# Crossbar keys, whole-tile stores and one more half group in an attention and feed-forward kernel

## The chip, the cores and the metric

One core of a Trainium2 chip. The metric is the device time of one execution in microseconds (us), median of several; a profiled execution's span is 1.7 to 2.1 us shorter than its time. TensorE is PE in the views, VectorE DVE, ScalarE ACT, GpSimd POOL; SP issues most stores and all turns by the crossbar (DMA transposes). A turn is a transposition; SBUF and PSUM are the memories that the kernel's tiles lie in. A transfer is cut into packets that up to 16 DMA engines carry, and the packet records show closing packets of 4 bytes, read here as one for each engine that takes part in a store (16 in the kernel before, where over the tail, from 234.6 to 239.0 us, 14.7 store packets moved at a time in the mean).

## The reference

```python
# attention: q, k, v are (8 batches, 8 heads, 576, 64); k and v are averaged over groups of 8 rows
k_p = k.reshape(B, H, 72, 8, D).mean(axis=3)
v_p = v.reshape(B, H, 72, 8, D).mean(axis=3)
attn = softmax(q @ k_p.T / 8)
x = (attn @ v_p).transpose(0, 2, 1, 3).reshape(4608, 512)
# feed-forward: w1, w2, w3 are (512, 768), w_out is (768, 512)
out = np.maximum(np.maximum(x @ w1, x @ w2), x @ w3) @ w_out     # (4608, 512) float32
```

## The kernel before

The feed-forward part runs in nine blocks of 512 tokens. A block yields control after each group of four matmuls ("slot"), and a plan says which attention steps of a later batch go into which slot. Query rows are held in nine interleaved groups, so a tile of 128 tokens is two groups of 64 rows, each of which goes to every ninth row of the output.

```python
NG = 9
GS = (0, 2, 4, 6, 8, 1, 3, 5, 7)          # order of the row groups in a batch
...
def turn_k(b):                             # keys: transposed by TensorE, copied out of PSUM
    pkt = keys(b, TR)                      # six TensorE transposes
    for par in range(2):
        fill_kz(b, par, 0, H, pkt,
                nc.scalar.copy if b == 1 else nc.vector.tensor_copy)
...
# x of batches 2 to 7 and q of batches 2 to 7 are turned by the crossbar, issued from SP
nc.sync.dma_start_transpose(out=xT[:, :, g0 + keep:g0 + 128], in_=...)
nc.sync.dma_start_transpose(out=qTs[b], in_=...)
...
# project(): one tile of 128 tokens leaves in two stores of 64 rows
for u in range(2):
    b, g = divmod(2 * m + u, NG)
    dst = out[S * b:S * b + S, :].rearrange("(r g) c -> r g c", g=NG)
    (nc.scalar if last and u else nc.sync).dma_start(
        out=dst[:, GS[g], c], in_=osb[64 * u:64 * u + 64, c])
...
# block 0 takes its columns in parts (first weight group, end, first column, end column)
parts = [(0, 1, 0, 128), (0, 1, 128, 256), (1, 2, 0, 256), (0, 2, 256, NB), (2, JCH, 0, NB)]
```

The softmax here doesn't subtract the row's maximum and nothing guards it: scores larger than these inputs give would overflow.

Of the kernel before, what the change touches and what calls it, by code (L numbers as in the profile page):

```python
# [14 lines left out]
def kernel(  # L15
# [11 lines left out]
    nc = tc.nc  # L27
    dt = mybir.dt
    F32, BF16, F16 = dt.float32, dt.bfloat16, dt.float16

    B, H, S, D = q.shape
# [10 lines left out]
    NG = 9  # L42
    GS = (0, 2, 4, 6, 8, 1, 3, 5, 7)
    NR = 64
    KCH = C // 128
    JCH = DFF // 128
    TOK = B * S
    NB = 512
# [4 lines left out]
    sb2 = ctx.enter_context(tc.tile_pool(name="sb2", bufs=2))  # L53
# [1 line left out]
    psp = ctx.enter_context(tc.tile_pool(name="psp", bufs=1, space=PSUM))  # L55
    ctx.enter_context(tc.manual_schedule())

    kts, vts, qbs, kps, qTs, ets = {}, {}, {}, {}, {}, {}

    def after(loads, first):  # L60
        for x in loads:
# [49 lines left out]
    for i in range(3):  # L111
# [6 lines left out]
        out=wo_sb, in_=moe_w_out.rearrange("(jc p) c -> p jc c", p=128))  # L118
# [25 lines left out]
    def fold_k(b, e, i0=0, i1=6):  # L144
        if b not in kps:
            new_kp(b)
        fold(e, kts[b][:, i0:i1], [kps[b][:, i0:i1, i, :] for i in range(2)])
# [12 lines left out]
    def turn_q(b, n0, n1, evac, tag):  # L160
        if b not in qTs:
            qTs[b] = sb2.tile([128, 2 * NG, 128], BF16, name="qT", tag="qT")
        pqt = psp.tile([128, n1 - n0, 128], BF16, name="pqt", tag=tag[0],
                       bufs=tag[1])
        qf = qbs[b].rearrange("p hp t d -> p (hp t d)")
        for n in range(n0, n1):
            nc.tensor.transpose(pqt[:, n - n0, :], qf[:, 128 * n:128 * n + 128],  # L167
                                ident)
        evac(out=qTs[b][:, n0:n1, :], in_=pqt)

    def keys(b, tag):
        pkt = psp.tile([128, 6, 96], BF16, name="pkt", tag=tag[0], bufs=tag[1])
        for i in range(6):
            nc.tensor.transpose(pkt[:, i, :], kps[b][:, i, :, :], ident[0:96, 0:96])  # L174
        return pkt

    def fill_kz(b, par, h0, h1, pkt, evac):
        rows = slice(64 * par, 64 * par + 64)
        evac(out=kz_all[b % 2][rows, par, h0:h1, 0:Sp].rearrange(  # L179
                 "p h (r i) -> p h r i", i=6),  # L180
             in_=pkt[rows, :, 12 * h0:12 * h1].rearrange("p i (h r) -> p h r i", r=12))

    def turn_k(b):
        pkt = keys(b, TR)
        for par in range(2):
            fill_kz(b, par, 0, H, pkt,
                    nc.scalar.copy if b == 1 else nc.vector.tensor_copy)

    def pool_k(b, tag):

        new_kp(b)
        pkp = psp.tile([128, 6, D], F32, name="pkp", tag=tag[0], bufs=tag[1])
        for j in range(4):
            nc.tensor.matmul(pkp, identh[0:96, :], k16[:, :, j, :],
                             start=(j == 0), stop=(j == 3))
        nc.vector.tensor_copy(out=kps[b][:, :, 0, :], in_=pkp[0:96])
        nc.scalar.copy(out=kps[b][:, :, 1, :], in_=pkp[0:96])
# [12 lines left out]
    def new_et(b):  # L210
        ets[b] = sb2.tile([Sp, H, S], F16, name="et", tag="et")

    def scores(b, h):
        psc = psp.tile([128, 1024], F32, name="psc", tag="att", bufs=2)
        score(b, h, psc[:, 0:320], 0, 0, 5)
        score(b, h, psc[:, 320:512], 1, 0, 3)
        score(b, h, psc[:, 512:576], 1, 3, 4)
        exp(ets[b][:, h, :], psc[0:Sp, 0:S])
# [33 lines left out]
    TR = ("tr", 1)  # L252
# [5 lines left out]
    def do(b, steps):  # L258




        for name in steps.split():
            i = int(name[1:] or 0)
            if name[0] in "qQ":
                turn_q(b, *QS[i], nc.vector.tensor_copy if name[0] == "Q"
                       else nc.scalar.copy, TR)
            elif name[0] == "T":
                qTs[b] = sb2.tile([128, 2 * NG, 128], BF16, name="qT", tag="qT")
                nc.sync.dma_start_transpose(  # L270
                    out=qTs[b], in_=qbs[b].rearrange("p hp t d -> p (hp t d)"))
            elif name[0] == "k":
                turn_k(b)
            elif name[0] == "K":
                pool_k(b, PW)
            elif name[0] == "a":
                nc.vector.tensor_tensor(out=k16, in0=kts[b][:, :, 0:4],
                                        in1=kts[b][:, :, 4:8], op=ALU.add)
            elif name[0] == "s":
                if i == 0:  # L280
                    new_et(b)
                scores(b, i)
            elif name[0] == "v":
                xns[b, i] = values(b, CHUNKS[i][0])
            else:
                turn_x(b, *CHUNKS[i], xns[b, i], TR,
                       nc.vector.tensor_copy if name[0] == "X" else nc.scalar.copy)
# [23 lines left out]
    def hidden(n, hT):  # L311

        parts = [(0, JCH, 0, NB)]
        if n == 0:
            parts = [(0, 1, 0, 128), (0, 1, 128, 256), (1, 2, 0, 256), (0, 2, 256, NB),
                     (2, JCH, 0, NB)]
        elif n == 1:
            parts = [(0, 1, 0, 256), (0, 1, 256, NB), (1, JCH, 0, NB)]
        for j0, j1, c0, c1 in parts:
            for jc in range(j0, j1):  # L320
                yield from hidden_part(n, jc, c0, c1, hT)

    def project(n, hT):
        for mm in range(4):
            m = 4 * n + mm
            last = m == TOK // 128 - 1
            osb = sb3.tile([128, C], F32, name="osb", tag="osb", bufs=5)
            for c in ((slice(0, C // 2), slice(C // 2, C)) if last else (slice(0, C),)):
                po = psp.tile([128, c.stop - c.start], F32, name="po", tag="pw", bufs=3)
                for jc in range(JCH):  # L330
                    nc.tensor.matmul(po, hT[:, jc, bass.ts(mm, 128)], wo_sb[:, jc, c],  # L331
                                     start=(jc == 0), stop=(jc == JCH - 1))
                if c.start:
                    nc.vector.tensor_copy(out=osb[:, c], in_=po)
                else:
                    nc.scalar.copy(out=osb[:, c], in_=po)  # L336
                for u in range(2):
                    b, g = divmod(2 * m + u, NG)
                    dst = out[S * b:S * b + S, :].rearrange("(r g) c -> r g c", g=NG)
                    (nc.scalar if last and u else nc.sync).dma_start(  # L340
                        out=dst[:, GS[g], c], in_=osb[64 * u:64 * u + 64, c])
            yield

    def new_hT():
        return sb2.tile([128, JCH, NB], F16, name="hT", tag="hT")
# [13 lines left out]
    for i in range(0, 6, 2):  # L359
        src = kts[0][:, i:i + 2] if i else kt0  # L360
        f = const.tile([96, 2, 4, D], F32, name="kf", tag="kf")
# [5 lines left out]
            out=kps[0][:, i:i + 2].rearrange("p i a d -> p a i d"),  # L367
# [64 lines left out]
    def block(n, plan):  # L432

        hT = new_hT()
        slot = 0
        for part in (hidden(n, hT), project(n, hT)):
            for _ in part:
                if slot == 0 and n > 0:
                    pool_work(n, mms[-1])
                for b, steps in plan.get(slot, ()):  # L440
                    if b < B:
                        do(b, steps)
                slot += 1

    fold_v(1)
    fold_k(2, nc.gpsimd)
    block(0, {0: [(0, "X1")], 3: [(0, "v2")], 5: [(0, "v3")], 6: [(0, "x2")],
              8: [(0, "x3")], 10: [(0, "v4")], 12: [(0, "x4")],
              13: [(1, "a")], 15: [(1, "K")], 17: [(1, "k")], 19: [(1, "Q0")],
              20: [(1, "Q1")], 21: [(1, "Q2 s0")], 22: [(1, "Q3 s1")],  # L450
              23: [(1, "s2 s3")], 24: [(1, "s4 s5")], 25: [(1, "s6 s7")],
              26: [(1, "v0")], 27: [(1, "v1 x0"), (2, "T")], 28: [(1, "v2 x1")],
              29: [(1, "v3 x2")], 30: [(1, "v4")]})


    def plan(n):
        b, i = n + 1, 3 * (n == 1)
        got = {0: [], 3: [], 3 + i: [(b, "k")]}
        got.update({5 + i + h: [(b, f"s{h}")] for h in range(H)})
        got[12 + i].append((b + 1, "T"))  # L460
        got.update({15 + i + c: [(b, f"v{c} x{c}")] for c in range(5)})
        if n == 1:
            got[0].append((1, "x3"))
            got[3].append((1, "x4"))
        return got

    def pool_work(n, mm):

        if n + 2 < B:
            after([load_k(n + 2)], mm)  # L470
            load_q(n + 2)
            load_v(n + 2)
        if n == 1:
            fold_v(2)
        if n + 2 < B:
            fold_k(n + 2, nc.gpsimd)
            fold_v(n + 2)
# [33 lines left out]
```

## Time and profile before

| | before |
|---|---|
| time, median of 3 | 242.86 us (242.78 to 244.19) |
| span of the profiled run | 241.0 us |
| block 0 / block 3 / block 7 | 31.7 / 24.4 / 20.7 us |
| last matmul to the end of the span | 4.4 us |

The lines that carry this stand in the prediction. A "block" here goes from its first feed-forward matmul to the next block's. TensorE is busy all through blocks 1 to 8 (24.28 of 24.28 us in block 2, 20.72 of 20.72 in block 7), so nothing but its own instructions bounds them.

### The profile page before, as it was taken

How to read it: one execution, taken by the hardware profiler on the slowest of the kernel's cores; microseconds unless marked ns; L12 is line 12 of the kernel's file. 1: busy time of each engine (PE TensorE's matmuls, PEld its weight loads, DVE VectorE, ACT ScalarE, POOL GpSimd, SP SyncE). 2: the span in 40 equal slices, each digit the busy share in tenths (PEclk: the TensorE clock that was granted, in tenths of full speed). 3: DMA queues.
4: the chain of work that ended last, by engine and by line, in shares of the span. 5: the costliest groups of instructions: out<-in, count | busy, mean ns of one | idle time of the engine just before them, and what ended most of it. 6: DMA issues, size and time to landing. Idle time of an engine off the chain costs nothing.

```text
span 241.0 us, 4221 instructions
## 1 busy us (share of the span) xinstructions
PE 230.9 (96%) x1609; PEld 122.7 (51%) x1609; DVE 131.7 (55%) x239; ACT 100.1 (42%) x173; POOL 123.7 (51%) x91
## 2 busy tenths in 40 slices
PE   7698999999999999999999999999999999999992
PEld 3376555575554555455545554555455544444441
DVE  6856754665583558354836483648364834504530
ACT  2373247546513651365235523552355232142121
POOL 8864276989997479638880979286500000000000
PEclk9999999999999999999999999999999999999999
DMA  7999999999948995699769987997640253043006
GB/s 135 188 198 206 196 202 208 169 166 241 184 97 153 222 166 120 128 194 197 131 125 156 227 176 133 193 192 135 133 93 0 69 123 85 3 108 66 0 20 154
DMA packets 51939, 34.29 MB, mean 142 GB/s; under 512 B 32144, under 2 KB 46480, under 8 KB 51920
## 3 DMA queue, kind: packets, MB, share of 16 engines
q0 software_dynamic: 17088, 17.11, 45.5%
q1 hardware_dynamic: 34672, 16.79, 34.3%
q8 instruction: 12, 0.20, 0.3%
q10 hardware_dynamic: 160, 0.13, 0.2%
q14 instruction: 7, 0.06, 0.1%
HBM read 34.60 MB, written 9.44 MB: 183 GB/s over the span
## 4 chain that ended last, share of the span: by engine, by line
PE 89%; DVE 5%; ACT 2%; DMA 2%; issue 1%; DVEq 0%
PE pw L295 55%; PE po L331 19%; PE psc L203 6%; PE pav L238 4%; DMA kt<-in_k_dram 2%; PE pxt L229 1%; DVE kf L362 1%; ACT et L208 1%; DVE t L304 1%; PE pkt L174 1%; PE pvp L156 1%; DVE xn L246 1%; PE pqt L167 1%; DVE kp L366 1%; DVE kf L364 1%
## 5 line engine op out<-in xcount | busy, mean ns | idle before, releaser
L295 PE MATMUL pw<-xT,mw 128*128 128x512 f16 (+2 forms) x696 | 155.6, 364 | 0.8 <-ACT xT L233 0.7
L295 PEld LDWEIGHTS <-mw 128*128 128x128 f16 x696 | 61.8, 98 | 56.2 <-issue 1.0
L304 DVE TENSOR_TENSOR t<-t,pw 128x512 f16<-128x512 f16 (+2 forms) x58 | 37.8, 651 | 71.0 <-PE pw L295 43.7
L301 ACT CAST t<-pw 128x512 f16<-128x512 f32 (+2 forms) x58 | 32.3, 556 | 56.1 <-PE pw L295 54.8
L331 PE MATMUL po<-mwo,hT 128*128 128x512 f16 (+1 forms) x222 | 50.7, 373 | 0.0
L208 ACT ACTIVATE et<-psc 72x576 f16<-72x576 f32 (+2 forms) x62 | 40.7, 662 | 20.9 <-PE psc L203 20.7
L307 DVE TENSOR_TENSOR hT<-t,pw 128x512 f16<-128x512 f16 (+2 forms) x58 | 37.7, 650 | 9.0 <-PE pw L295 5.3
L336 ACT COPY osb<-po 128x512 f32<-128x512 f32 (+1 forms) x36 | 20.9, 580 | 47.7 <-PE po L331 43.7
L135 POOL TENSOR_TENSOR half<-vt 72x2048 f32<-72x2048 f16 x7 | 28.4, 4060 | 10.0 <-DMA vt<-in_v_dram 9.9
L331 PEld LDWEIGHTS <-hT 128*128 128x128 f16 x222 | 20.3, 97 | 21.3 <-DVE hT L307 2.4
L135 POOL TENSOR_TENSOR half<-kt 96x1536 f32<-96x1536 f16 x6 | 18.5, 3085 | 23.4 <-DMA kt<-in_k_dram 23.3
L246 DVE TENSOR_TENSOR xn<-pav,rcp 128x512 f16<-128x512 f32 x39 | 27.0, 691 | 1.5 <-DVE rcp L244 0.2
L136 POOL TENSOR_TENSOR half<-half 72x1024 f32<-72x1024 f32 (+1 forms) x13 | 27.2, 2096 | 1.0
L203 PE MATMUL psc<-qT,kz 128*128 128x64 bf16 (+3 forms) x192 | 25.9, 246 | 0.4 <-DVE kz L179 0.3
L203 PEld LDWEIGHTS <-kz 128*128 128x128 bf16 x192 | 17.8, 98 | 15.7 <-DVE kz L179 1.5
L238 PEld LDWEIGHTS <-et 72*128 72x128 f16 x312 | 15.2, 98 | 7.6
L238 PE MATMUL pav<-vp,et 72*128 72x65 f16 x312 | 16.5, 194 | 0.0
L244 DVE RECIPROCAL rcp<-pav 128x8 f32<-128x8 f32 x39 | 7.9, 204 | 9.4 <-PE pav L238 9.3
L139 POOL TENSOR_TENSOR kp<-half 96x384 bf16<-96x384 f32 x12 | 11.7, 993 | 0.5
L179 DVE COPY kz<-pkt 64x576 bf16<-64x576 bf16 (+1 forms) x14 | 9.9, 711 | 2.9 <-PE pkt L174 2.7
L79 POOL DMA_DIRECT2D vt<-in_v_dram x10 | 8.0, 804 | 2.9 <-DMA qb<-in_q_dram 2.2
L139 POOL TENSOR_TENSOR vp<-half 72x512 f16<-72x512 f32 x7 | 8.9, 1268 | 0.5
(48 smaller groups left out, 79.1 us busy)
## 6 DMA issues: line engine op xcount, KB each, us to landing
out_dram<-osb SPq DMA_DIRECT2D x70, 128.0 KB, 2.4
kt<-in_k_dram POOLq DMA_DIRECT2D x7, 576.0 KB, 7.4
qb<-in_q_dram POOLq DMA_DIRECT2D x7, 576.0 KB, 12.2
vt<-in_v_dram POOLq DMA_DIRECT2D x7, 576.0 KB, 15.0
mw<-in_moe_w_dram POOLq DMA_DIRECT2D x9, 256.0 KB, 9.3
mwo<-in_moe_w_out_dram POOLq DMA_DIRECT2D x1, 768.0 KB, 18.1
qb<-in_q_dram POOLq DMA_DIRECT2D x2, 288.0 KB, 7.0
xT<-xn SPq DMA_TRANSPOSE x30, 2.4
```

Source lines behind the costliest of these rows:

```text
L135: e.tensor_tensor(out=f, in0=t[:, :, 0:4, :], in1=t[:, :, 4:8, :], op=ALU.add)
L136: e.tensor_tensor(out=f[:, :, 0:2, :], in0=f[:, :, 0:2, :], in1=f[:, :, 2:4, :], op=ALU.add)
L203: nc.tensor.matmul(out, kz_all[b % 2][:, f % 2, h, :], qTs[b][:, n + i0:n + i1, 64 * (h % 2):64 * (h % 2) + 64], start=True, stop=True)
L208: nc.scalar.activation(out=out, in_=in_, func=FT.Exp, scale=1.0 / 64.0)
L238: nc.tensor.matmul(pav[:, h // 4, 65 * (h % 4):65 * (h % 4) + 65], ets[b][:, h, c0:c0 + 128], vp_all[:, b, h, :], start=True, stop=True)
L246: nc.vector.tensor_tensor(out=xn, in0=pv[:, :, :, 0:D], in1=rcp.to_broadcast([128, 2, 4, D]), op=ALU.mult)
L295: mm = nc.tensor.matmul(pw, w_sb[wi][:, kc, bass.ts(jc, 128)], xT[:, kc, col], start=(kc == 0), stop=(kc == KCH - 1))
L301: nc.scalar.copy(out=t, in_=pw)
L304: nc.vector.tensor_tensor(out=t1, in0=t, in1=pw, op=ALU.max)
L307: nc.vector.tensor_tensor(out=hT[:, jc, c0:c1], in0=t, in1=pw, op=ALU.max)
L331: nc.tensor.matmul(po, hT[:, jc, bass.ts(mm, 128)], wo_sb[:, jc, c], start=(jc == 0), stop=(jc == JCH - 1))
L336: nc.scalar.copy(out=osb[:, c], in_=po)
```

## The change

The intent is to take the key transposes off TensorE, to store a tile with one instruction instead of two where its row groups allow it (a "joined store"), and to give the first block more work between the last turn of its tokens and their use: block 0 works on halves of its 512 columns at first, and the "half group" is one more group of weights taken in halves.

```diff
 def turn_k(b):
-    pkt = keys(b, TR)
+    pkt = keys(b, TR) if b < 3 else kTs[b]
     for par in range(2):
-                nc.scalar.copy if b == 1 else nc.vector.tensor_copy)
+                nc.vector.tensor_copy if b == 2 else nc.scalar.copy)
+elif name[0] == "Z":
+    kTs[b] = sb2.tile([128, 6, 96], BF16, name="kT", tag="kT")
+    nc.sync.dma_start_transpose(out=kTs[b], in_=kps[b].rearrange("p i a d -> p (i a d)"))
 ...
-parts = [..., (1, 2, 0, 256), (0, 2, 256, NB), (2, JCH, 0, NB)]
+parts = [..., (1, 3, 0, 256), (0, 3, 256, NB), (3, JCH, 0, NB)]
 ...
+e = nc.scalar if last and c.start == 0 else nc.sync
+b, g = divmod(2 * m, NG)
+dst = out[S * b:S * b + S, :].rearrange("(r g) c -> g r c", g=NG)
+if g < NG - 1 and GS[g] < GS[g + 1]:
+    step = GS[g + 1] - GS[g]
+    e.dma_start(out=dst[GS[g]:GS[g + 1] + 1:step, :, c], in_=osb[:, c])   # 28 of 36 tiles
+    continue
 for u in range(2):                     # the other eight tiles as before
 ...
-# keys copied at slot 3, values from slot 15 (blocks 2 to 8)
+# keys copied at slot 2, values from slot 14, next batch's keys turned at slot 17
```

The plan of block 0 is stretched from 31 slots to 34.

## The prediction

> **What bounds the kernel now.** I read the page's busy table and chain first, then one repeating block in a table of stretches and in the timeline, then the first block, the tail and the transfers.
>
> ```profile
> PE 230.9 (96%) x1609; PEld 122.7 (51%) x1609; DVE 131.7 (55%) x239; ACT 100.1 (42%) x173; POOL 123.7 (51%) x91
> ...
> PE 89%; DVE 5%; ACT 2%; DMA 2%; issue 1%; DVEq 0%
> ```
>
> TensorE is busy 96% and holds 89% of the chain. A busy PE may still hide stalls, so I add up one block by hand. The stretches (start:end, length, then busy time by engine) show equal blocks:
>
> ```profile
> 22.70:48.85 26.15, 25.40 (x214) 15.35 (x214) 14.23 (x28) 13.22 (x25) 16.32 (x10) 1.00 1.23 191
> ...
> 97.88:122.25 24.37, 24.37 (x168) 12.49 (x166) 13.81 (x24) 10.73 (x18) 15.63 (x11) 1.00 0.96 165
> ...
> 195.07:215.79 20.72, 20.72 (x98) 9.40 (x96) 8.26 (x12) 5.86 (x10) 0.00 (x0) 1.00 0.30 67
> ```
>
> Block 7 (195.07 to 215.79) has feed-forward work alone: 96 matmuls of 512 columns in 20.72, 0.216 us each. A middle block adds 8 score groups of 0.25, 5 value groups of 0.26 and one key turn of 0.26 (chain, timeline): 20.7 + 2.0 + 1.3 + 0.26 = 24.26, against 24.3 measured. So blocks 1 to 8 have no stall worth naming; only fewer PE instructions can shorten them.
>
> Block 0 is different. It runs from 17.30 to 48.85, 31.55 us. Its work is 20.7 feed-forward, about 1.7 for the end of batch 0 and 5.8 for batch 1 (pooling matmuls 0.65, key turn 0.25, q turns 1.0, scores 2.0, values 1.3, x turns 0.66): 28.2. So 3.3 us stall, nearly all before 27.4:
>
> ```profile
> 20.42 1.04 PE L295 MATMUL pw<-xT,mw 128*128 128x256 f16 x8
> 21.62 0.40 PE L229 MATMUL pxt<-identh,xn 128*128 128x128 f16 x4 [0.16 <-DVE xn L246]
> 22.69 1.03 PE L295 MATMUL pw<-xT,mw 128*128 128x256 f16 x8 [0.67 <-ACT xT L233]
> ```
>
> The second half of the columns is wanted straight after chunk 3 is turned.
>
> The tail: PE ends at 236.5, the span at 241.0. Eight stores leave SP at about 0.6 us each; the last is issued near 237.9, about 0.9 after its data is ready (DVE copy 236.56 + 0.42).
>
> ```profile
> 233.27 5.17 SPq L340 DMA_DIRECT2D out_dram<-osb  x8
> ...
> 236.56 0.42 DVE L334 COPY osb<-po 128x256 f32<-128x256 f32 x1 [4.51 <-PE po L331]
> ```
>
> Last the transfers (count, KB each, median us to landing):
>
> ```profile
> out_dram<-osb SPq DMA_DIRECT2D x70, 128.0 KB, 2.4
> kt<-in_k_dram POOLq DMA_DIRECT2D x7, 576.0 KB, 7.4
> ...
> xT<-xn SPq DMA_TRANSPOSE x30, 2.4
> ...
> qT<-qb SPq DMA_TRANSPOSE x6, 5.9
> ```
>
> Stores and crossbar turns share the SP queue. A 128 KB store lands in 2.4 us because it is spread: the packet records show 64 packets of 2,048 bytes and 16 closing packets of 4 bytes per store, one close for each of 16 engines.
>
> [...]
>
> **The change, part by part.**
>
> Keys: five turns of six transposes leave PE, 5 x 0.26 = 1.3 us off the path. Five crossbar turns of 108 KB are added to SP, before chunk 4's turn; SP is busy about 15 us of a 24 us block and the pooled keys are ready (POOL ends them at 113.56 in the block begun at 97.88, the turn comes near 119). The copies go to ACT (0.63 each, 10.7 of 24.3 busy) from DVE, earlier, without waiting for PE. Hidden.
>
> Half group: twelve matmuls become 24 of half width[...]. It puts three more half groups (1.3 us of PE work) between chunk 3's turn and its use. Walking the measured durations through the new order, PE starts the second column half about 0.35 later than now but with 1.3 us more done: 0.95 gained; spreading batch 1's scores and values over 34 slots instead of 31 gains perhaps 0.5 more, of the 3.3 available. The key pooling of batch 1 still waits for its DVE add of 0.95 us. I take 1.4.
>
> Stores: 28 of 36 tiles go out in one instruction, saving SP issue time that is hidden, except in the tail: up to 0.9 us. But the listing of the built kernel shows the new destination as 2x64x512, source 128 rows. [...]k = 2: the whole 256 KB tile goes through two of 16 engines, 64 packets of 2 KB on each. This is the term that decides.
>
> A 2 KB store packet lasts 81 ns at the shortest, 96 typically beside loads, and about 150 when 16 engines write together (packet records). I take 96: 64 x 0.096 = S = 6.1 us per tile[...], where a tile took some 1.2 on all. A batch's k, q and v loads read 3.54 MB of float32, a sixteenth per engine is 221 KB; at the 25.8 GB/s of the first key load's packets (4,096 bytes in 159 ns), 8.6 us. A batch's crossbar turns (1.29 MB, 80 KB per engine, 256 bytes in 18 ns) take 5.7. A middle block now asks [...]3 x 6.1 + 8.6 + 5.7 = 32.6 us, in a block in which PE needs 24.0. [...]the turns of q and x queue behind the previous block's stores in SP's ring, and the next block starts only when its x chunks have landed. So the two engines become the bound.
>
> Estimate, step by step:
> - Block 0 ends near 47.2, its three joined stores begin on the engines near 43.9. Block 2 starts when they (18.3), a batch of loads (8.6), q and three x turns (4.0) and landing (1) are through: 75.8.
> - Blocks 2, 3 and 4 each carry three stores of the block before: 32.6 + 0.9 for landing = 33.5 each, to 176.3. Block 5 carries block 4's four: 39.6, to 215.9.
> - Block 6 carries two and no loads: PE-bound, 24; blocks 7 and 8: 20.7 each. PE ends near 281.
> - Block 8's four tiles (its last in two halves) are issued from about 277.5: 4 x 6.1 + 3 to start and land: span 305, time (span + 1.8) 307.
> With S = 5.4 (84 ns) the same sums give 292; with loads and stores overlapping on an engine (load time halved) 15 to 20 less. I centre on 296.
>
> **Rivals.**
> - The hardware spreads a store over 16 engines in spite of its leading 2 (or splits the longer side). Then it is just the gains: 1.3 + 1.4 + 0.6 = 3.3, 239.5 us. For it: old stores of the same rows are spread.[...] 8%.
> - Two engines, but blocks absorb it: loads lie half a block ahead and turns have some slack, so just the tail pays: 4 S + 3 from 230 gives a span near 257, time 259. Against it: the per-block sum above PE's time.
> - Two engines and packets at the slow 150 ns: S = 9.6, time beyond 350. Against it: that duration belongs to 16 writers sharing one limit (about 220 GB/s in the tail's slices).
> - SP becomes late through longer crossbar or store issues with all engines in use: its 15 us of 24 leaves room; at most 1 us.
>
> **Range and chances.** 264 to 328 spans overlapped engine work at 84 ns and nearly additive work at 115 ns. Faster by over 2% needs below 238.0, beyond even the first rival's sum: 2%. Within 2% is the first rival: 8%. Slower: 90%.
>
> **What would show each step.** Two closing packets instead of 16 per joined store, and a landing of 7 us or more instead of 2.4: right on k. PE idle at block starts, waiting for xT's turns, blocks 2 to 5 at 30 us or more and block 7 still 20.7: right on the mechanism. A DMA share that stays low while PE waits: two engines, not all. A span that ends some 20 us after the last matmul: the tail. Key turns missing from PE and no waits on kz: the keys. Stores still landing in about 2.5 us and blocks of 24.0 would make me wrong altogether.

## The result, and the profile after

The changed kernel takes 320.13 us (319.46 to 323.07, 4 runs) against 242.82 us (242.40 to 244.19) for the kernel before. The ratio is 1.319, 95% interval 1.310 to 1.329. Ratios here are the mean time of one kernel's runs over that of the other's of the same rounds, so not quite the ratio of the medians. Executions over 1.5% slower than the fastest of the same kernel are left out of the means.

From the page, busy times and the chain that ended last:

```profile
PE 242.3 (76%) x1591; PEld 125.4 (39%) x1591; DVE 122.6 (39%) x230; ACT 112.1 (35%) x185; POOL 123.2 (39%) x91
...
PE 64%; SPq 13%; DMA 9%; DVE 3%; issue 2%; ACT 2%; DVEq 0%
```

TensorE fell from 89% of the chain to 64%. SP's queue and transfers, 2% together before, now hold 22%.

Stretches of the profile after (start:end, length, busy times of PE, PEld, DVE, ACT, POOL, the granted clock, DMA share, GB/s), for blocks 2, 6 and 7:

```profile
80.52:117.52 37.00, 25.79 (x161) 12.64 (x162) 12.14 (x22) 12.95 (x20) 16.66 (x10) 0.87 0.83 113
...
226.85:254.64 27.79, 26.18 (x160) 12.63 (x161) 12.14 (x22) 12.33 (x19) 0.00 (x0) 0.94 0.41 80
254.64:275.36 20.72, 20.72 (x97) 9.39 (x96) 8.24 (x12) 5.85 (x10) 0.00 (x0) 1.00 0.17 56
```

Block 7, without attention, is unchanged at 20.72. Block 2 went from 24.3 to 37.0. What TensorE waited for at the start of block 3, in its timeline (start, length, then in brackets the idle time and its releaser), and in the table of waits (total, times, longest):

```profile
117.52 7.06 PE L299 MATMUL pw<-xT,mw 128*128 128x512 f16 x24 [11.03 <-DMA xT<-xn]
```

```profile
PE pw L299 <- DMA xT<-xn: 39.6, 4, 14.9
```

The turn of x was late because of what stood before it. SP's own queue over block 2 (start, length, operation, count):

```profile
80.63 1.22 SPq L274 DMA_TRANSPOSE kT<-kp  x1
81.94 2.27 SPq L352 DMA_DIRECT2D out_dram<-osb  x2
84.31 1.56 SPq L223 DMA_TRANSPOSE xT<-xn  x1
85.96 12.48 SPq L346 DMA_DIRECT2D out_dram<-osb  x3
98.54 13.69 SPq L270 DMA_TRANSPOSE qT<-qb  x1
112.33 5.15 SPq L223 DMA_TRANSPOSE xT<-xn  x4
```

Three joined stores hold SP for 12.48 us and the turn of q behind them for 13.69, where a store took about 0.6 and that turn about 3.7 before. The four turns of x are issued after it, 1.3 us apart. The same stores (four of 64 rows) and turn in the kernel before:

```profile
76.11 3.48 SPq L340 DMA_DIRECT2D out_dram<-osb  x4
86.41 3.70 SPq L270 DMA_TRANSPOSE qT<-qb  x1
```

The transfers (count, KB each, landing where the page could count one):

```profile
out_dram<-osb SPq DMA_DIRECT2D x27, 256.0 KB
kt<-in_k_dram POOLq DMA_DIRECT2D x7, 576.0 KB, 15.0
```

The page gives no landing for the joined stores any more; the loads of k land in 15.0 us instead of 7.4. The packet records tell why: SP's queue has 2,320 four-byte closing packets before and 1,640 after. One load (16), 41 turns (32 each) and 16 stores of 64 rows (16 each) make 1,584; the remaining 56 are 28 joined stores with two closing packets each. Two engines carry a tile: over the tail, from 297.5 to 315.0 us, 2.1 store packets moved at a time in the mean, and the DMA share from 297.0 to 315.5 was 0.13 of the 16 engines. The packet records also show what held the turn of q. From 96 to 100 us 46 store and 50 load packets moved, so the two engines took stores and loads by turns; from 101.2 to 111.5 it was 258 store packets of 84 ns each in the median, no load, and 469 of the turn's packets, all within 0.6 us. The rest of the turn moved from 111.78 on, when the last store packet was done (111.80).

The tail, last line of SP's timeline:

```profile
293.01 8.51 SPq L346 DMA_DIRECT2D out_dram<-osb  x4
```

The last matmul ends at 296.3 and the span at 317.7: 21.4 us of tail instead of 4.4.

### The profile page after: what moved, and what is told of

Its sections match the earlier page's. It is cut to its first block, busy times and chain, and to the rows that moved or that the text cites. A ratio compares the mean times of both kernels' runs of the same rounds, so it can differ in the third digit from the quotient of the medians.

```text
span 317.7 us, 4171 instructions
## 1 busy us (share of the span) xinstructions
PE 242.3 (76%) x1591; PEld 125.4 (39%) x1591; DVE 122.6 (39%) x230; ACT 112.1 (35%) x185; POOL 123.2 (39%) x91
## 4 chain that ended last, share of the span: by engine, by line
PE 64%; SPq 13%; DMA 9%; DVE 3%; issue 2%; ACT 2%; DVEq 0%
PE pw L299 40%; PE po L335 13%; SPq L270 8%; PE psc L203 5%; SPq L223 5%; DMA qT<-qb 4%; PE pav L238 3%; DMA xT<-xn 2%; DMA kT<-kp 2%; ACT kz L179 1%; DMA kt<-in_k_dram 1%; DVE kf L373 1%; PE pqt L167 1%; PE pvp L156 1%; DVE kp L377 0%
## 5 line engine op out<-in xcount | busy, mean ns | idle before, releaser
L299 PE MATMUL pw<-xT,mw 128*128 128x512 f16 (+2 forms) x708 | 166.5, 378 | 46.0 <-DMA xT<-xn 39.6
L299 PEld LDWEIGHTS <-mw 128*128 128x128 f16 x708 | 65.1, 101 | 109.1 <-issue 62.0
L335 PE MATMUL po<-mwo,hT 128*128 128x512 f16 (+1 forms) x222 | 49.6, 373 | 0.0
L208 ACT ACTIVATE et<-psc 72x576 f16<-72x576 f32 (+2 forms) x62 | 40.7, 662 | 21.4 <-PE psc L203 21.4
L179 ACT COPY kz<-kT 64x576 bf16<-64x576 bf16 x10 | 11.6, 1164 | 8.2 <-DMA kT<-kp 8.1
L72 POOL DMA_DIRECT2D kt<-in_k_dram x9 | 5.1, 565 | 16.3 <-PE pw L299 14.7
```

What stands on the lines that cost most here:

```text
L208: nc.scalar.activation(out=out, in_=in_, func=FT.Exp, scale=1.0 / 64.0)
L299: mm = nc.tensor.matmul(pw, w_sb[wi][:, kc, bass.ts(jc, 128)], xT[:, kc, col], start=(kc == 0), stop=(kc == KCH - 1))
L335: nc.tensor.matmul(po, hT[:, jc, bass.ts(mm, 128)], wo_sb[:, jc, c], start=(jc == 0), stop=(jc == JCH - 1))
```

## The experiments

Twelve kernels ran, all with correct results. Block lengths are differences of the start times of the blocks' first matmuls in the traces.

**1. The old stores in the changed kernel.** The joined branch is replaced by the loop of before.

> The changed kernel with the old stores, two per tile, each of 64 rows on both sides (16 engines). Theory (joined stores on two engines are the whole loss): 239.5 us, 238.5 to 240.5; middle blocks 24.0 us, block 0 about 0.9 shorter than before, no wait of TensorE on the x turns. Rival (the crossbar turns of the keys, or the order on the SP queue, cost the time): above 300 us.

Measured 242.25 us against 243.19 of before (ratio 0.995, interval 0.987 to 1.002, so a gain is not shown by this run alone). The profile is as expected: blocks of 24.02, block 0 of 30.8, no wait on a turn.

```profile
96.86:120.88 24.02, 24.02 (x161) 12.29 (x160) 12.15 (x22) 13.07 (x20) 16.66 (x11) 1.00 0.96 174
```

So keys, half group and the new plan are not what costs the time.

**2. The joined stores in the kernel before**, nothing else.

> The kernel before with the joined stores alone. Theory: 310 to 330 us, two closing packets per joined store, block starts waiting for the x turns, a tail of some 21 us after the last matmul. Rival (joined stores are harmless without the keys on the crossbar): under 250 us.

Measured 314.76 us, ratio 1.294, with two closing packets per joined store again (SP's 1,480 less 1,424 leave 56 for 28) and a tail of 21.8 us. Block 2:

```profile
81.55:118.21 36.66, 25.85 (x166) 12.74 (x167) 13.89 (x24) 10.73 (x18) 16.64 (x10) 0.87 0.90 110
```

The joined stores alone make nearly the whole loss. The other 5 us of the changed kernel appear only beside them, in blocks 4 to 6 (2.9, 2.0 and 1.1 us longer).

**3. Joined stores over 16 engines.** VectorE writes the hidden tile's columns with the two row groups interleaved (its write then has a step of two elements), so that a store's partitions count row pairs and the slowest destination dimension is 64:

```diff
-nc.vector.tensor_tensor(out=hT[:, jc, c0:c1], in0=t, in1=pw, op=ALU.max)
+nc.vector.tensor_tensor(
+    out=hT[:, jc, c0:c1].rearrange("p (m r u) -> p m u r", r=64, u=2),
+    in0=t.rearrange("p (m u r) -> p m u r", r=64, u=2),
+    in1=pw.rearrange("p (m u r) -> p m u r", r=64, u=2), op=ALU.max)
 ...
-dst = out[...].rearrange("(r g) c -> g r c", g=NG)
-e.dma_start(out=dst[GS[g]:GS[g + 1] + 1:step, :, c], in_=osb[:, c])
+dst = out[...].rearrange("(r g) c -> r g c", g=NG)
+e.dma_start(out=dst[:, GS[g]:GS[g + 1] + 1:step, c], in_=osb[:, c])
```

> The changed kernel, still one store per joined tile, but with the tile's rows laid out so that the destination's slowest dimension is 64 instead of 2[...]. Theory: 238.5 to 240.5 us, landing near 2.5 us, blocks of 24.0, and a tail shorter than the old stores' by up to 0.9 us. Rival (a joined store is slow because it is one large transfer of 256 KB): above 300 us.

Measured 240.68 us, ratio 0.988 (0.982 to 0.995). The same 256 KB in one instruction is harmless when 64 comes first instead of 2:

```profile
out_dram<-osb SPq DMA_DIRECT2D x27, 256.0 KB, 4.4
```

Landing is 4.4 us in the median, not the 2.5 expected, but off the path. The tail is 3.5 us instead of 4.4, and the closing packets are back at 16 per joined store.

**4. Stores of 51 and 13 row pairs.** As 3, but each joined tile leaves as 51 and 13 row pairs.

```diff
-e.dma_start(out=dst[:, GS[g]:GS[g + 1] + 1:step, c], in_=osb[:, c])
+for r0, r1 in ((0, 51), (51, 64)):
+    e.dma_start(out=dst[r0:r1, GS[g]:GS[g + 1] + 1:step, c], in_=osb[2 * r0:2 * r1, c])
```

> As the run with the rows laid out anew, but each joined tile leaves as 51 and 13 of the 64 row pairs: [...]at most 36 packets of 2 KB on one engine instead of 64 or 8. Theory (what counts is the sum of work on the busiest engine per block): 3 tiles x 36 x 0.084 us = 9.1, loads 8.6, turns 5.7: 23.4 us, just under the 24.0 that TensorE needs, so blocks of 24.0 to 25.5; the last four tiles need 12 us on the busiest engine, so a tail near 10 us: 242 to 252 us in all. Rival (anything under 16 engines costs the same large price): above 300 us.

The 36 packets are the estimate: 34 on each of 3 engines for the 51 pairs and 2 on each of 13 for the rest. Those counts divide 51 and 13, as the closing packets measured in other runs divide theirs (2 for a leading 2, 16 for 64, 22, read as 7 + 15, for 49 and 15). How many engines carried this run's stores was not shown.

Measured 282.91 us, ratio 1.163: neither, and the tail is 13.7 us instead of near 10. The price lies between those of the changed kernel, with 64 packets on each of two engines (1.319), and of experiment 3, with 8 on each of 16 (0.988), but there is no free ground below TensorE's 24 us in this run. SP's queue over block 2 of this run:

```profile
76.07 1.22 SPq L274 DMA_TRANSPOSE kT<-kp  x1
77.39 2.15 SPq L355 DMA_DIRECT2D out_dram<-osb  x2
79.64 1.42 SPq L223 DMA_TRANSPOSE xT<-xn  x1
81.16 5.42 SPq L349 DMA_DIRECT2D out_dram<-osb  x6
88.81 12.43 SPq L270 DMA_TRANSPOSE qT<-qb  x1
101.33 6.09 SPq L223 DMA_TRANSPOSE xT<-xn  x4
```

The joined stores start 5.2 us after the block does (75.9), behind the turns of keys and of x. From their start to the end of q's turn it is 20.1 us, about the estimated 9.1 of stores and 8.6 of loads and a turn, one after the other. Then three turns of x, 1.3 apart, and a landing: the next block starts at 107.5. The estimate "sum of work on the busiest engine" left out some 5 us at either end, when the turns are paced by SP and waited for one by one. This is arithmetic on one block; experiment 9 puts it to a test.

**5. TensorE kept warm.** `heat(...)` with 15, 48, 24, 43 and 64 filler matmuls at the ends of blocks 1 to 5.

> The changed kernel with filler matmuls of 512 columns (15, 48, 24, 43, 64) at the ends of blocks 1 to 5, as long as TensorE's idle times there, so that its clock should not fall. Its trace lost some 12 us of TensorE time to a lower clock after idle times. If that loss lies on the path: 308 to 312 us. If the two engines' queue sets the block times and TensorE only waits longer when it is quicker: 316 to 322 us, with at most 3 us gained in block 6, the only block after a wait that no store holds up.

The reason to try it: after its wait, block 3's 24 matmuls took 7.06 us in the changed kernel, where 24 take 5.18 at 0.216 each. In the trace, after 11.03 us of waiting the first eight matmuls stand 0.43 us apart (3.4 us), the later ones 0.216, so 1.9 us were lost. Measured 321.35 us, ratio 1.314. Stretches of blocks 2 and 3:

```profile
84.11:120.22 36.11, 34.65 (x208) 16.98 (x209) 12.15 (x22) 13.05 (x20) 16.67 (x10) 1.00 0.79 115
120.22:152.24 32.02, 29.39 (x184) 14.60 (x185) 12.15 (x22) 13.05 (x20) 13.85 (x9) 0.99 1.13 127
```

The clock was 1.00 and 0.99 instead of 0.87 and 0.93, and the blocks were as long as before (36.1 and 32.0 against 37.0 and 31.6); block 6, where up to 3 us might have been gained, took 28.2 against 27.8. The lower clock is a sign of the waits, not a part of the loss.

**6 and 7. Joined stores in the last block only, and in all blocks but the last.**

```diff
-if g < NG - 1 and GS[g] < GS[g + 1]:
+if n == TOK // NB - 1 and g < NG - 1 and GS[g] < GS[g + 1]:     # 6; in 7: n < TOK // NB - 1
```

> The changed kernel with joined stores in the last block alone. Theory (the tail's share is the last block's four tiles on two engines, 4 x 64 x 0.084 = 21.5 us instead of 4.6 after the last matmul): 256 to 260 us, all blocks as in the run with the old stores. Rival (the tail only carries backlog from earlier blocks): under 250 us.

> The changed kernel with joined stores in all blocks but the last. Theory: 320 less the tail's 17: 302 to 305 us, span ending 5 to 7 us after the last matmul. Rival (tail and blocks share one backlog, so sparing one helps less): above 310 us.

Measured 258.36 us (ratio 1.060) and 303.48 us (ratio 1.246). In 6 the blocks are as in experiment 1 and the tail is 21.5 us; in 7 the tail is 4.6 us and the blocks are as in the changed kernel. So the tail costs 17 us and the blocks the rest, and the two add.

**8. All stores but the last half tile on ScalarE's queue**, so that no turn stands behind a store in SP's queue.

```diff
-e = nc.scalar if last and c.start == 0 else nc.sync
+e = nc.sync if last and c.start else nc.scalar
```

> The changed kernel with all stores but the last half tile issued from ScalarE, so that they have a ring of their own and the turns are no longer queued behind them on SP; the same two engines carry them. If the loss is mostly the turns' place in the queue behind the stores: 265 to 295 us (the two engines' total work still fills about 225 us from 43 on). If it is the two engines' bandwidth alone: 305 to 330 us. ScalarE may be held while it issues, which would spoil the gain; its waits will show that.

Measured 342.29 us, ratio 1.402: worse. The expectation's own warning came true. From the table of waits, and the longest single issue in ScalarE's queue:

```profile
ACT t L305 <- issue: 33.2, 5, 12.2
```

```profile
201.19 12.03 ACTq L346 DMA_DIRECT2D out_dram<-osb  x1
```

One store holds ScalarE for 12.03 us, and with it the casts that TensorE's buffers need. SP's turns of q were still held (10.4 us at 109.74), though no store was in their queue. The packet records show why: from 118 to 125 us stores and turns moved side by side, 21 store and 172 turn packets a us, where turns without stores move over 1,000 a us in this trace (128 to 129). So a queue of their own let the turns start, and the two busy engines still held them. The held ScalarE spoils the comparison of the times, so how many us each part is worth stays open.

**9. Seven and fifteen engines**: as 4, with 49 and 15 row pairs.

> As the run with 51 and 13 row pairs, but 49 and 15: [...]at most 14 + 2 = 16 packets of 2 KB on one engine per joined tile (8 with all 16 engines, 36 before, 64 in the changed kernel). Serial chain (turns at both ends of a block, some 11 us, with stores and loads one after the other between): a three-tile block needs 5.3 + 3 x 16 x 0.084 + 8.6 + 1.6 + 5.2 = 24.7 us, 0.7 over what TensorE needs, and 244 to 250 us in all. Straight line through the runs with 8, 36 and 64 packets (1.4 us of time per packet): about 252. Threshold at TensorE's 24.0 us by the sum of work alone: 240 to 242.

Measured 258.36 us, ratio 1.066: above all three. The closing packets are 22 per joined tile (616 of SP's 2,200, by the count used above), read here as 7 + 15. But even an estimated 16 packets on the busiest engine (98 over 7 and 30 over 15) instead of 8 move blocks 2 to 6 to between 24.7 and 29.0 us and the tail to 7.8. The three-tile blocks 2 to 4, for which the serial chain gave 24.7, took 26.4, 24.7 and 27.5, so that sum is not confirmed. ScalarE's timeline at the start of block 6 (178.14) shows a wait that none of the three theories had:

```profile
181.62 1.23 SPq L274 DMA_TRANSPOSE kT<-kp  x1
182.94 1.19 SPq L355 DMA_DIRECT2D out_dram<-osb  x2
184.04 2.33 ACT L179 COPY kz<-kT 64x576 bf16<-64x576 bf16 x2 [4.26 <-DMA kT<-kp]
...
185.25 0.31 PE L203 MATMUL psc<-qT,kz 128*128 128x320 bf16 x1 [1.77 <-ACT kz L179]
...
186.40 0.59 ACT L305 CAST t<-pw 128x512 f16<-128x512 f32 x1
```

The key turn is issued behind the turns of x, so when these slip, it lands late. Its copies stand in ScalarE's program ahead of the casts; ScalarE waits 4.26 us for the turn, copies for 2.33, and only then serves the cast of 186.40 that TensorE's matmuls wait for. So the key turn's lateness became a stall of the feed-forward part. ScalarE waits for it up to 4.3 us in each of five blocks of this run (10.9 in the table of waits); what the copies' place is worth was not tested by a run of its own.

**10. The half group alone in the kernel before** (the two lines of block 0, parts and plan).

> The kernel before with the half group and its plan of the first block alone. Theory: block 0 shorter by 0.9 us, the rest as before: 0.9 us faster (ratio 0.994 to 0.998). Rival (the gain in block 0 only moves a wait into block 1): ratio 0.999 to 1.001.

Measured 241.73 us against 242.81, ratio 0.997 (0.994 to 0.999). Block 0 is 30.82 instead of 31.73 and later blocks are unchanged: a small but real gain, and it stays.

**11 and 12. Experiments 3 and 1 again, in five rounds on one chip.**

> The 16-engine joined stores once more, timed in more rounds: ratio 0.982 to 0.990 (half group 0.9, keys 1.3, tail 0.9 us of 243).

> The old stores with keys and half group once more, in more rounds beside the run above: ratio 0.987 to 0.994, and 0.6 to 1.2 us slower than the 16-engine joined stores, all of it in the tail.

Measured 240.64 us (ratio 0.991, 0.989 to 0.993) and 241.27 us (ratio 0.994, 0.991 to 0.997). Both beat the kernel before, the 16-engine joined stores by 0.9%. Their lead of 0.6 us on the old stores is less than the spread of either's runs, though their tail is 1.0 us shorter in the traces (3.6 against 4.6). The first ratio lies just outside what was expected, the second at its slow end: the median times gained 2.2 us where the profiled spans (238.3 against 241.0) gained 2.7.

## Why the prediction was right or wrong

- **That two engines carry a joined store, and that this decides: right.** Two closing packets per joined store, 16 with a leading 64, 22 with 49 and 15 pairs; experiments 2 and 3 show the joined stores as the cause and the leading dimension as the reason.
- **The time inside the range (264 to 328), the centre 24 us low.** That it lies inside is in part luck: with packets of 84 ns the steps give 292, and the range reaches 320 only by its allowance for packets of 115 ns, which did not come. The term mis-sized is "32.6 + 0.9 for landing" per middle block. Packets took 84 ns, not 96 (median of the trace; mean 99), so three tiles are 16.1 us instead of 18.3 and the step's sum 31.4 instead of 33.5. Yet blocks 2, 3 and 4 took 37.0, 31.6 and 37.1 us (only block 3 fits it), block 1 32.9 where the steps give 28.6, block 5 40.6 where they give 39.6, and block 6 27.8 where they give 24. The step took stores as starting before the block and turns as engine time alone. In block 2 SP reached the joined stores 5 us after the block's start, behind the turns of keys and x. Their packets moved from 91.5 to 111.8: 20.3 us for 16.1 of stores, as the two engines took loads by turns with them, and begun 5.5 us after SP's issue, behind packets of the two other stores and of a turn of x that moved beside loads. Then came q's turn and 5 us of x turns one by one. Experiment 4, designed on the same sum, missed by 31 us; its block 2 shows the same order. The packet records, with those of experiment 8, show both parts of the wait: in one queue the turns stood behind the stores, and in a queue of their own they moved slowly beside them. How many us each is worth is not settled.
- **The tail: right in kind, 21.4 us where the step gave about 24**, with 84 ns in place of 96. The second rival ("just the tail pays", 259) was wrong as a whole, but experiment 6 makes its case and measures 258.4. That the two agree so closely is luck: the rival took 27.4 us after 230, and it was 21.5 after 234.1.
- **The key copies "hidden": right with 16 engines, wrong beside late turns.** "0.63 each" was the copy from PSUM; from SBUF it takes 1.16 (median of ten), both with a step of 192 bytes. Why the second takes longer was not shown, as no run here varies the step or the source alone. In experiment 1 nothing waits for these copies; in the changed kernel ScalarE waits 8.1 us in all, in experiment 9 10.9. Block 6 of the changed kernel is late by this: the key turn lands at 233.0, its two copies end at 235.4, and only then comes the cast that TensorE's matmul of 236.06 waits for.
- **Keys worth 1.3 us: right.** Blocks 2 to 6 took 121.5 us before and 120.1 in experiment 1, 1.4 less.
- **The half group worth 1.4: wrong by a third.** It measured 0.9. The walk through the new order gave 0.95; the "0.5 more" for the stretched plan did not come: the key pooling waits 0.34 us and the key turn 0.28 in the run of experiment 3.
- **Tail gain of up to 0.9 from one issue per tile: right**, once all engines take part (4.4 to 3.5).
- **The first rival (239.5 with 16 engines)** is about experiment 3, which reached 240.7.
- **The 150 ns of the third rival: read wrongly.** The prediction gave them to 16 writers that share one limit. In experiment 3 all 16 engines write, and a packet takes 91 ns in the median, against 147 in the kernel before. One thing that differs is that a store has 128 rows instead of 64; no run varies this alone.
- **Left out altogether: the clock.** The granted mean was 0.895 against 0.998 before. It fell, as the waits made it, and experiment 5 shows that it did not matter: with 1.00 and 0.99 in blocks 2 and 3 instead of 0.87 and 0.93, the kernel took 321.35 us against 320.13.

## What to carry to other kernels

Before joining two transfers into one, look at the slowest dimension of both sides as the built program has it: here a leading 2 put all of a 256 KB store on two engines (two closing packets; 64 packets of 84 ns on each, 5.4 us, and 20.3 us instead of 16.1 for three tiles with loads between). If rows must interleave, lay them out so that the long dimension comes first: with 64 in front the same store had 16 closing packets and landed in 4.4 us. And a transfer that nothing waits for can set the time all the same, once the turns behind it in the queue, or beside it on its engines, feed the next block: q's turn took up to 15.1 us to issue with stores on two engines, against 3.4 to 4.6 in the kernel before.
